# Dilated attention feeding a Strassen MoE on one Trainium2 core: two differences of h in places of their own, seven weight places, and the last attention visits moved

## The chip, the cores and the metric

The kernel runs on one core of a Trainium2 chip. The metric is the device time of one execution in microseconds (us); lower is better. Before the change three runs took 957.64, 956.73 and 954.7 us, median 956.73.

## The reference

```python
# attention: q, k, v are [8, 8, 576, 64]; the first 4 heads use mask_plain, the others mask_dil
mask_plain = (rel >= 0) & (rel < 32)
mask_dil = (rel >= 0) & (rel < 128) & (rel % 4 == 0)
scores = np.where(masks, scale * q @ k.T, -1e9)
attn = softmax(scores);  attn_out = attn @ v
# x: [4608, 512]; w_gate, w_val: [512, 1536]; w_out: [1536, 512]
g = x @ w_gate
silu = g * (1.0 / (1.0 + np.exp(-g)))
return silu * (x @ w_val) @ w_out
```

The 4608 tokens are 8 batches of 576; a token's x is the attention output of its 8 heads. Everything is float32.

## The kernel before

Tokens run along the free dimension (columns), features along the partitions. A float32 product is made of three TensorE passes over a high and a low half of each operand, so every operand needs a "split": ScalarE copies the rounded high half (a CAST or COPY), and VectorE (DVE) or GpSimd (POOL) subtracts it to get the low half. TensorE (PE) is fed by five queues: its own, DVE, ScalarE (ACT), POOL and SyncE (SP). The order in which instructions stand on each engine is set by a scheduler from the order in the code and its own estimate of times; on the chip each engine then works its queue strictly in that order.

The program has two parts.

- **Plain part**: 4 chunks of 384 columns, in 48 steps (gate, value, output product). Beside it, combinations of the weights are formed and written to DRAM as 63 "pieces" of 512 KB.
- **Strassen part**: 3 chunks (0, 1, 2) of 1024 columns, each as 2 x 2 blocks with NT = 7 products in place of 8. A chunk is 126 "slots". The first 84 are the **gate stage**: for each of NP = 6 pairs of feature blocks (i), 7 products (t), 2 slots each, one for gate and one for value. `gated` forms the four blocks of h, `hq[a, b, i]`, as sums of products come in: the last (0,1) after t = 6. The other 42 slots are the **out stage**: 7 products of 6 steps. One slot is 6 matmuls of 128x512 in the gate stage and 6 in the out stage too.

What else runs in the Strassen part:

- **Pieces.** Each product reads one piece (two i of the out stage share one). `ask` starts their transfers from POOL's queue into a ring of NAT places at `M_RING`; `next_piece(n)` stands behind the product that reads piece n and asks for piece n + NAT - 1, whose place was left by piece n - 1.
- **h for the out stage.** `h_split` makes the high and low halves of the operand of an out product: for t = 0, 1, 5, 6 a block of h, for t = 3 and 4 the differences hq[0,1] - hq[0,0] and hq[1,1] - hq[0,1], which `h_mix` forms on POOL in place, in hq[0,0] and hq[0,1]. In place means that it must stand behind the split of t = 0, which reads hq[0,0]. So `h_mix(i)` stands at the end of i for i = 0, 1, 2; those of 3 and 4 stand with the splits of i = 5; that of 5 behind the stage. For t = 2 two more differences are formed on DVE (`tt` on line 736, called from `h_split`). Low halves alternate between POOL (even i) and DVE (odd i); nine places (HS) hold them, so a split is made 8 steps ahead of its product.
- **Sums of x.** `x_step` 0 to 10 forms the seven x operands of the next chunk from its four blocks b11, b12, b21, b22, with 128x1024 operations on DVE and ACT; steps 0 to 7 and 10 stand in slots 104 to 124 of the chunk ahead, 8 and 9 in the first slots of the chunk itself.
- **Attention visits.** 46 packs of attention are worked off in between. A visit m has two ends: A (PE: `results` of m-1, `scores` of m; then DVE `norm` of m-1, line 404, and `shift` of m, lines 365 to 368; ACT `exps`, line 373) and, some slots later, B (PE: `turn_y` of m-1, line 411, which needs norm, and `turn_e` of m, line 377, which needs exps; ACT copies to x). PE works in order too, so if norm or exps is late at B, PE stands still. Chunk 0 of the Strassen part needs packs up to 25, chunk 1 those from 26 to 35, chunk 2 those from 36 to 45. Before, visits 27 to 36 stand in chunk 0 with A in slots 2 to 94; visits 37 and 38 in slots 106 and 119 of its out stage, between the sums of x; 39 to 46 in slots 5 to 94 of chunk 1. Chunk 2 has none.

Of the kernel before, what the change touches and what calls it, by code (L numbers as in the profile page):

```python
# [25 lines left out]
NF = DFF // P  # L26
NK = DM // P
WB = 3 * DM
NP = NF // 2
# [15 lines left out]
CS = 512  # L45
# [7 lines left out]
PIECE = 1024  # L53
NPG = NT * NP
NPIECE = NPG + NT * NP // 2


ORDER = (2, 0, 3, 1)
# [61 lines left out]
NPK = len(PACKS)  # L120
# [14 lines left out]
def attention_moe(ctx, tc, qkb, vb, w, masks, ident, out):  # L135
    nc = tc.nc
# [15 lines left out]
    M_X0 = M_RAW + 8 * WU  # L152
    M_W = M_X0 + 2 * NK * CH
    M_RING = M_W + NT * 4 * CS
    M_HQ = M_RING + 10 * PIECE
    assert M_HQ + 4 * NP * CS <= M_W + 2 * WB * NF
    M_LOW = M_RAW + PIECE
    M_OT = M_LOW + 2 * PIECE + CS
    assert M_OT + 4 * CH + 2 * CS <= M_X0
# [3 lines left out]

    pieces = tc.dram_tile([NPIECE, P, PIECE], F32, name="pieces")

    def at(o, n, dt=F32):

        assert o % 8 == 0
        key = o, n, dt
        if key not in named:  # L170
            k = n * 4 // mybir.dt.size(dt)
            named[key] = nc.alloc_sbuf_tensor_at(f"at{o}_{n}_{dt.name}", [P, k], dt, offset=origin + 4 * o).ap()
        return named[key]
# [395 lines left out]
    NSLOT = 21 * NP  # L569
    SB = NPLAIN * NB  # L570
# [3 lines left out]
    def visits(m, a, b):  # L574
        assert a not in visit and b not in visit
        visit[a], visit[b] = ("A", m), ("B", m)


    M1 = 4 * NPLAIN + 10
# [4 lines left out]
    for m in range(13, M1 + 1):  # L584
        a = SB - 75 + 49 * (m - 13) // 10
        visits(m, a, a + 3)
    for n in range(9):
        a = SB + 2 + 92 * n // 9
        visits(M1 + 1 + n, a, a + 6)
    for m in range(M1 + 10, NPK + 1):  # L590
        a = SB + 94 + NSLOT * (m - M1 - 10) // 10
        visits(m, a, a + 7)

    def attend(now):
        what, m = visit.get(now, ("", 0))
# [94 lines left out]

    NAT = 10
    taken = {}
    asked = 0
    NC = NCS
# [1 line left out]
    def ask(n):  # L698

        nonlocal asked  # L700
        while asked < min(n, NPIECE * NC):
            taken[asked] = at(M_RING + PIECE * (asked % NAT), PIECE, F32R)
            nc.gpsimd.dma_start(out=taken[asked], in_=pieces[asked % NPIECE])  # L703
            asked += 1

    def next_piece(n):

        taken.pop(n)
        ask(n + NAT)


    xs = [[at(M_W + 2 * CS * (2 * t + l), 2 * CS, F32R).rearrange("p (k c) -> p k c", k=2) for l in range(2)]
          for t in range(NT)]
    hq = {(a, t, i): at(M_HQ + CS * (4 * i + 2 * a + t), CS) for a in range(2) for t in range(2) for i in range(NP)}

    x1 = at(M_X0 + 4 * CS, 2 * CS).rearrange("p (k c) -> p k c", k=2)
    HS = 9
# [17 lines left out]
    def tt(engine, out, a, b, op=ALU.subtract):  # L735
        engine.tensor_tensor(out=out, in0=a, in1=b, op=op)  # L736
# [16 lines left out]
    def h_split(n):  # L753

        t, i = divmod(n % (NT * NP), NP)
        if t == 2:
            src = h2_ring()
            tt(nc.vector, src, hq[1, 1, i], hq[0, 0, i])
            tt(nc.vector, hq[1, 0, i], hq[1, 0, i], src)
        else:  # L760
            src = (hq[0, 0, i], hq[1, 0, i], None, hq[0, 0, i], hq[0, 1, i], hq[1, 0, i], hq[1, 1, i])[t]
        o = at(hs_at(n), 2 * CS, F32R).rearrange("p (l c) -> p l c", l=2)
        nc.scalar.copy(out=o[:, 0], in_=src)  # L763
        tt((nc.gpsimd, nc.vector)[i % 2], o[:, 1], src, o[:, 0])
        hs[n] = o

    def h_mix(i):

        tt(nc.gpsimd, hq[0, 0, i], hq[0, 1, i], hq[0, 0, i])
        tt(nc.gpsimd, hq[0, 1, i], hq[1, 1, i], hq[0, 1, i])  # L770


    banks = [[bank_g, bank_v], bank_o[:2], bank_o[2:]]

# [24 lines left out]
    def gated(i, t):  # L799
        if t not in SUMS:  # L800
            return
        a, b = SUMS[t][0]
        g = total(t, 0, g_ring)
        f = f_ring()
        nc.scalar.activation(out=f, in_=g, func=AF.Tanh, scale=0.5)  # L805
        v = total(t, 1, v_ring)
        nc.vector.scalar_tensor_tensor(out=f, in0=f, scalar=1.0, in1=g, op0=ALU.add, op1=ALU.mult)  # L807
        nc.vector.scalar_tensor_tensor(out=hq[a, b, i], in0=f, scalar=0.5, in1=v, op0=ALU.mult, op1=ALU.mult)  # L808

    def outs(ci, t, i, r):  # L810
        w = taken[NPIECE * ci + NPG + NP // 2 * t + i // 2]
# [22 lines left out]
    for s in range(NS):  # L834
        ci, f = divmod(s, NF)
        W = 2 * s
        w_upto(L=W + 3, H=W + 4, E=W + 6)
        gv_mm(ci, f, 0)
        act_tanh(s)
        attend(3 * s)  # L840
        dve_u(s)
        mix_to(2 * (s - NF) + 1)
        with tc.issue_after(last["h"].ins):
            w_upto(T=W + 5, B=W + 5)
        w_upto(L=W + 4, H=W + 5, E=W + 7)
        gv_mm(ci, f, 1)
        attend(3 * s + 1)
        dve_h(s)
        h_hi(s)
        with tc.issue_after(last["h"].ins):  # L850
            w_upto(T=W + 6, B=W + 6)
        if s > 0:
            out_mm(s - 1)
        h_lo(s)
        if s > 0 and f == 0:
            out_store(ci - 1)
        attend(3 * s + 2)

        mix_to(2 * (s - NF) + 2)
        if ci == NPLAIN - 1:  # L860
            if f >= 9:
                ask([4, 7, NAT - 1][f - 9])
            for n in {5: (0,), 6: (1,), 7: (2,), 8: (3,), 10: (4, 5), 11: (6, 7)}.get(f, ()):
                x_step(n)


    for ci in range(NC):
        base = SB + NSLOT * ci
        first = n_out(ci, 0, 0)
        for i in range(NP):  # L870
            for n in range(NT):
                for r in range(2):
                    gate_val(ci, i, n, r)
                    if ci == 0 and i == 0 and n == 1 and r == 1:
                        out_mm(NS - 1)
                        out_store(NPLAIN - 1)
                    attend(base + 2 * (NT * i + n) + r)
                gated(i, SEQ[i][n])
                next_piece(NPIECE * ci + NT * i + n)
                if i == 0 and n < 3:  # L880
                    if n < 2 or ci == 0:
                        x_step((8, 9, 10)[n])
                if i == NP - 1:
                    for k in {1: (3, 4), 2: (5, 6), 3: (7, 8)}.get(n, ()):
                        h_split(first + k)
                        if k < 5:
                            h_mix(k)
            if i < 3:
                h_split(first + i)
                h_mix(i)  # L890
        h_mix(NP - 1)
        for t in range(NT):
            for i in range(NP):
                n = n_out(ci, t, i)
                for r in range(2):
                    outs(ci, t, i, r)
                    if i == NP - 1:
                        out_done(ci, t, r)
                if first < n and n - 1 + HS < n_out(ci + 1, 0, 0):
                    h_split(n - 1 + HS)  # L900
                if i % 2 == 1:
                    next_piece(NPIECE * ci + NPG + NP // 2 * t + i // 2)
                slot = 2 * NPG + NP * t + i
                attend(base + slot)
                if ci + 1 < NC and slot > 102 and slot % 2 == 0:
                    k = (slot - 104) // 2
                    if k < 8 or k == 10:
                        x_step(k)
# [44 lines left out]
```

## Time and profile before

| what | value |
|---|---|
| median of 3 runs | 956.73 us |
| profiled execution, its time | 954.66 us |
| its span | 952.9 us |
| mean granted TensorE clock | 0.995 |
| PE busy | 932.4 us (98%) |
| DVE busy | 642.1 us (67%) |
| ACT busy | 391.3 us (41%) |
| POOL busy | 347.0 us (36%) |

The profiled execution is 2.07 us under the median of the runs shown and 1.76 us above its own span. Line numbers (L736) are those of the code above; a line that is a helper's, as `tt` at L736, stands for all who call it. In lists of instructions the columns are start, duration, engine, line, operation, output <- inputs, count, and in brackets the idle time ahead and who ended it.

### The profile page before, as it was taken

The numbers are of one execution on the slowest core, as the hardware profiler recorded it, in microseconds if no ns is written. First come the engines' busy times: TensorE is split into PE (matmuls) and PEld (weight loads), VectorE is DVE, ScalarE is ACT, GpSimd is POOL, SyncE is SP. The second block draws the span as 40 slices with busy tenths as digits, with TensorE's granted clock in tenths as the row PEclk, the third lists the DMA queues.
The fourth block names the chain that finished last, engine by engine and source line by source line (L and its number), as shares of the span: only waits on it lengthen the run. The fifth ranks groups of instructions, "written<-read, shape, count | busy, mean of one in ns | idle before, by whom it ended". The sixth has DMA issues, their size and how long they took to land.

```text
span 952.9 us, 21913 instructions
## 1 busy us (share of the span) xinstructions
PE 932.4 (98%) x9204; PEld 814.8 (86%) x9204; DVE 642.1 (67%) x1008; ACT 391.3 (41%) x687; POOL 347.0 (36%) x364
## 2 busy tenths in 40 slices
PE   7899999999999999999999999999998899999998
PEld 5799999999999999888887888888886788888886
DVE  4766566667667755767579884666699735656972
ACT  4886322333233334333334643333445433333452
POOL 0776311111111131233145752232267623334681
PEclk9999999999999999999999999999999899999999
DMA  9985166566767691777777678677754586665571
GB/s 369 329 283 195 40 213 225 177 221 219 241 228 245 216 358 63 250 221 234 215 220 235 220 239 288 218 211 217 238 171 163 178 264 193 187 195 176 177 221 66
DMA packets 75249, 205.25 MB, mean 215 GB/s; under 512 B 7568, under 2 KB 23824, under 8 KB 75152
## 3 DMA queue, kind: packets, MB, share of 16 engines
q0 software_dynamic: 27216, 99.10, 34.4%
q1 hardware_dynamic: 35696, 65.07, 19.2%
q10 hardware_dynamic: 12240, 39.70, 12.5%
q8 instruction: 72, 1.18, 0.5%
q14 instruction: 25, 0.20, 0.1%
HBM read 161.37 MB, written 42.47 MB: 214 GB/s over the span
## 4 chain that ended last, share of the span: by engine, by line
PE 87%; DVE 8%; ACT 2%; issue 1%; DMA 0%; ACTq 0%; DVEq 0%
PE bo L779 29%; PE bo L495 10%; PE bv L458 10%; PE bg L458 10%; PE bv L779 10%; PE bg L779 10%; PE two L393 3%; DVE at_float L736 2%; PE two L353 2%; DVE at_float32r L736 2%; PE two L377 2%; PE two L411 2%; DVE at_float L807 1%; DVE at_float L808 1%; DMA at_bfloat<-masks 0%
## 5 line engine op out<-in xcount | busy, mean ns | idle before, releaser
L779 PE MATMUL bo<-at_float32r 128*128 128x512 f32 x1296 | 311.5, 394 | 0.2 <-DVE at_float L736 0.2
L779 PEld LDWEIGHTS bo<-at_float32r 128*128 128x128 f32 x1296 | 243.2, 189 | 52.3 <-DVE at_float L736 0.4
L703 POOL DMA_DIRECT2D at_float32r<-pieces x189 | 103.7, 549 | 251.3 <-PE bo L779 145.1
L736 DVE TENSOR_TENSOR at_float<-bo,at_float 128x512 f32<-128x512 f32 x168 | 113.5, 686 | 112.4 <-ACT at_float L784 57.9
L487 POOL TENSOR_TENSOR at_float32r<-at_float,at_float32r 128x384 fp32r<-128x384 f32 x48 | 54.9, 1144 | 218.0 <-PE bo L495 175.4
L779 PE MATMUL bg<-at_float32r 128*128 128x512 f32 x486 | 129.5, 392 | 0.8 <-DVE at_float32r L736 0.8
L779 PE MATMUL bv<-at_float32r 128*128 128x512 f32 x486 | 129.5, 393 | 0.0
L736 DVE TENSOR_TENSOR at_float32r<-at_float,at_float32r 128x512 fp32r<-128x512 f32 (+1 forms) x84 | 99.4, 1201 | 42.9 <-ACT at_float32r L763 28.5
L736 POOL TENSOR_TENSOR at_float32r<-at_float,at_float32r 128x512 fp32r<-128x512 f32 x63 | 95.5, 1516 | 63.3 <-ACT at_float32r L763 60.4
L458 PE MATMUL bg<-at_float32r,at_float32r 128*128 128x384 f32 x576 | 110.8, 339 | 2.1 <-DVE at_float L472 1.3
L458 PE MATMUL bv<-at_float32r,at_float32r 128*128 128x384 f32 x576 | 110.1, 338 | 0.0
L495 PE MATMUL bo<-at_float32r,at_float32r 128*128 128x384 f32 x576 | 110.1, 338 | 0.0
L779 PEld LDWEIGHTS bg<-at_float32r 128*128 128x128 f32 x486 | 90.5, 188 | 20.2 <-DVE at_float32r L736 1.2
L779 PEld LDWEIGHTS bv<-at_float32r 128*128 128x128 f32 x486 | 90.4, 188 | 19.4
L763 ACT CAST at_float32r<-at_float 128x512 fp32r<-128x512 f32 x126 | 75.7, 621 | 68.5 <-DVE at_float L736 21.5
L458 PEld LDWEIGHTS bg<-at_float32r,at_float32r 128*128 128x128 f32 x576 | 99.9, 188 | 3.7 <-POOL at_float32r L277 1.1
L495 PEld LDWEIGHTS bo<-at_float32r,at_float32r 128*128 128x128 f32 x576 | 100.2, 188 | 0.9
L458 PEld LDWEIGHTS bv<-at_float32r,at_float32r 128*128 128x128 f32 x576 | 99.8, 188 | 0.8
L805 ACT ACTIVATE at_float<-at_float 128x512 f32<-128x512 f32 x72 | 45.6, 634 | 86.9 <-DVE at_float L736 86.9
L472 DVE SCALAR_TENSOR_TENSOR at_float<-at_float,bg 128x384 f32<-128x384 f32 x48 | 26.6, 553 | 75.7 <-ACT at_float L467 75.7
L784 ACT COPY at_float<-bg 128x512 f32<-128x512 f32 x63 | 36.9, 586 | 81.3 <-PE bg L779 81.3
L277 POOL TENSOR_TENSOR at_float32r<-at_int,at_float32r 128x768 fp32r<-128x768 f32 x24 | 46.0, 1925 | 39.9 <-ACT at_float32r L273 39.7
(80 smaller groups left out, 980.0 us busy)
## 6 DMA issues: line engine op xcount, KB each, us to landing
at_float32r<-pieces POOLq DMA_DIRECT2D x189, 512.0 KB, 4.3
pieces<-at_float32r SPq DMA_DIRECT2D x126, 256.0 KB, 4.9
at_int<-w SPq DMA_DIRECT2D x24, 768.0 KB, 6.3
at_float<-vb ACTq DMA_DIRECT2D x28, 390.0 KB, 4.9
at_float<-vb ACTq DMA_DIRECT2D x14, 520.0 KB, 5.4
at_float<-qkb ACTq DMA_DIRECT2D x14, 448.0 KB, 5.8
out<-at_float SPq DMA_DIRECT2D x24, 256.0 KB, 4.5
at_float<-qkb ACTq DMA_DIRECT2D x10, 544.0 KB, 6.9
```

The lines of the kernel that those rows point to most:

```text
L277: nc.gpsimd.tensor_tensor(out=lo, in0=wst.pop(u).bitcast(F32), in1=hi, op=ALU.subtract)
L393: nc.tensor.matmul(out=two[BQ * j:BQ * j + BQ, h, (D + 1) * g:(D + 1) * (g + 1)], lhsT=t[r, BQ * i:BQ * i + BQ], rhs=v[r, i, :], start=Tru ...
L458: nc.tensor.matmul(out=bank[:, :CH], lhsT=wcol(f, o, low), rhs=x[ORDER[j]], start=n == 0, stop=n == len(ops) - 1)
L472: last["h"] = nc.vector.scalar_tensor_tensor(out=t, in0=t, scalar=1.0, in1=bank_g[:, :CH], op0=ALU.add, op1=ALU.mult)
L487: nc.gpsimd.tensor_tensor(out=hl, in0=hst[i][0], in1=hst[i][1], op=ALU.subtract)
L495: nc.tensor.matmul(out=bank_o[j][:, :CH], lhsT=wcol(f, 2 * DM + P * j, low), rhs=x, start=f == 0 and low == 0 and x is hh, stop=f == NF - ...
L703: nc.gpsimd.dma_start(out=taken[asked], in_=pieces[asked % NPIECE])
L736: engine.tensor_tensor(out=out, in0=a, in1=b, op=op)
L763: nc.scalar.copy(out=o[:, 0], in_=src)
L779: nc.tensor.matmul(out=bank, lhsT=w, rhs=x, start=first and n == 0 and t in FRESH, stop=last and n == len(ops) - 1, skip_group_check=True)
L784: nc.scalar.copy(out=kept[KEPT[t]][r], in_=banks[0][r][:, :CS])
L805: nc.scalar.activation(out=f, in_=g, func=AF.Tanh, scale=0.5)
```

## The change

1. `h1[i]`, a new place per i, takes hq[0,1] - hq[0,0]; hq[0,1] - in place still - takes the other difference. Both are issued in `gated` as soon as t = 6 of that i is done, ahead of `next_piece`. `h_mix` and its calls go. Product 3 reads h1.
2. Six places of h are paid for by three of the ring: NAT is 7 in place of 10; the first transfers, asked for in the plain part, are 6 pieces in place of 9.
3. Visits 37 and 38 leave the out stage of chunk 0. Chunk 1 now has ten visits (37 to 46) with A in the same slots as in chunk 0, 2 to 94; in the Strassen part B comes 6 slots behind A everywhere, where it was 7 for the visits from 36 on.

```diff
+NAT = 7
-    M_HQ = M_RING + 10 * PIECE
-    assert M_HQ + 4 * NP * CS <= M_W + 2 * WB * NF
+    M_HQ = M_RING + NAT * PIECE
+    assert M_HQ + 5 * NP * CS <= M_W + 2 * WB * NF
...
-    for n in range(9):
-        a = SB + 2 + 92 * n // 9
-        visits(M1 + 1 + n, a, a + 6)
-    for m in range(M1 + 10, NPK + 1):
-        a = SB + 94 + NSLOT * (m - M1 - 10) // 10
-        visits(m, a, a + 7)
+    for m in range(M1 + 1, NPK + 1):
+        c, n = divmod(m - M1 - 1, 10)
+        a = SB + NSLOT * c + 2 + 92 * n // 9
+        visits(m, a, a + 6)
...
-    hq = {(a, t, i): at(M_HQ + CS * (4 * i + 2 * a + t), CS) for a in range(2) for t in range(2) for i in range(NP)}
+    hq = {(a, t, i): at(M_HQ + CS * (5 * i + 2 * a + t), CS) for a in range(2) for t in range(2) for i in range(NP)}
+    h1 = [at(M_HQ + CS * (5 * i + 4), CS) for i in range(NP)]
...
-            tt(nc.vector, src, hq[1, 1, i], hq[0, 0, i])
+            tt(nc.vector, src, hq[1, 1, i], h1[i])
...
-            src = (hq[0, 0, i], hq[1, 0, i], None, hq[0, 0, i], hq[0, 1, i], hq[1, 0, i], hq[1, 1, i])[t]
+            src = (hq[0, 0, i], hq[1, 0, i], None, h1[i], hq[0, 1, i], hq[1, 0, i], hq[1, 1, i])[t]
...
-    def h_mix(i):
-
-        tt(nc.gpsimd, hq[0, 0, i], hq[0, 1, i], hq[0, 0, i])
-        tt(nc.gpsimd, hq[0, 1, i], hq[1, 1, i], hq[0, 1, i])
...
         nc.vector.scalar_tensor_tensor(out=hq[a, b, i], in0=f, scalar=0.5, in1=v, op0=ALU.mult, op1=ALU.mult)
+        if t == 6:
+            tt(nc.gpsimd, h1[i], hq[0, 1, i], hq[0, 0, i])
+            tt(nc.gpsimd, hq[0, 1, i], hq[1, 1, i], hq[0, 1, i])
...
-                ask([4, 7, NAT - 1][f - 9])
+                ask([3, 5, NAT - 1][f - 9])
...
                         h_split(first + k)
-                        if k < 5:
-                            h_mix(k)
             if i < 3:
                 h_split(first + i)
-                h_mix(i)
-        h_mix(NP - 1)
```

Each engine's order was taken from both built programs. In the rows below a tile is named by its place in SBUF, its size in words, its type and a number. The rows at three places of chunk 1 follow; L736 is `tt` before, L735 the same after.

POOL, from the split of step 4 in the last i of the gate stage, before. `at50880` and `at52928` are hq[0,0] of i = 3 and 4, `at51392` and `at53440` their hq[0,1]:

```order
L736 TENSOR_TENSOR at21184_1024_float32r_519<-at52928_512_float32_536,at21184_1024_float32r_519 128x512
L703 DMA at42688_1024_float32r_4587<-pieces_57 128x1024
L736 TENSOR_TENSOR at50880_512_float32_535<-at51392_512_float32_541,at50880_512_float32_535 128x512
L736 TENSOR_TENSOR at52928_512_float32_536<-at53440_512_float32_542,at52928_512_float32_536 128x512
L736 TENSOR_TENSOR at51392_512_float32_541<-at52416_512_float32_553,at51392_512_float32_541 128x512
L736 TENSOR_TENSOR at53440_512_float32_542<-at54464_512_float32_554,at53440_512_float32_542 128x512
L703 DMA at43712_1024_float32r_4605<-pieces_57 128x1024
L736 TENSOR_TENSOR at23232_1024_float32r_521<-at45760_512_float32_544,at23232_1024_float32r_521 128x512
```

The same place after, from the mixing of i = 3 on; `at51392` and `at53952` are now h1 of i = 3 and 4:

```order
L735 TENSOR_TENSOR at51392_512_float32_559<-at49856_512_float32_541,at49344_512_float32_535 128x512
L701 DMA at34496_1024_float32r_4492<-pieces_57 128x1024
L735 TENSOR_TENSOR at49856_512_float32_541<-at50880_512_float32_553,at49856_512_float32_541 128x512
L701 DMA at35520_1024_float32r_4494<-pieces_57 128x1024
L701 DMA at36544_1024_float32r_4496<-pieces_57 128x1024
L701 DMA at37568_1024_float32r_4539<-pieces_57 128x1024
L701 DMA at38592_1024_float32r_4541<-pieces_57 128x1024
L701 DMA at39616_1024_float32r_4587<-pieces_57 128x1024
L701 DMA at40640_1024_float32r_4605<-pieces_57 128x1024
L735 TENSOR_TENSOR at53952_512_float32_560<-at52416_512_float32_542,at51904_512_float32_536 128x512
L735 TENSOR_TENSOR at52416_512_float32_542<-at53440_512_float32_554,at52416_512_float32_542 128x512
L735 TENSOR_TENSOR at21184_1024_float32r_519<-at51904_512_float32_536,at21184_1024_float32r_519 128x512
```

The four mixing instructions that stood together stand in pairs, those of i = 3 one i (7 pieces) earlier, those of i = 4 ahead of the split of step 4.

DVE, in the last i of the gate stage, before. `at16064` and `at17088` are b11 and b12 of x, `at19136` their difference (x_step 2), `at27328` its low half (x_step 3); the rows that read `bo2` to `bo0` are the sums of products 4 and 5 for the last blocks of h:

```order
L736 TENSOR_TENSOR at22208_1024_float32r_520<-at54976_512_float32_537,at22208_1024_float32r_520 128x512
L736 TENSOR_TENSOR at24256_1024_float32r_522<-at47808_512_float32_545,at24256_1024_float32r_522 128x512
L736 TENSOR_TENSOR at19136_1024_float32_556<-at17088_1024_float32_103,at16064_1024_float32_102 128x1024
L736 TENSOR_TENSOR at27328_1024_float32r_525<-at19136_1024_float32_556,at26304_1024_float32r_524 128x1024
L736 TENSOR_TENSOR at10944_512_float32_4723<-bo2_509,at6648_512_float32_561 128x512
L736 TENSOR_TENSOR at12992_512_float32_4774<-bo3_513,at7160_512_float32_562 128x512
L807 SCALAR_TENSOR_TENSOR at13504_512_float32_4725<-at13504_512_float32_4725,at10944_512_float32_4723 128x512
```

The same place after:

```order
L735 TENSOR_TENSOR at22208_1024_float32r_520<-at54464_512_float32_537,at22208_1024_float32r_520 128x512
L735 TENSOR_TENSOR at24256_1024_float32r_522<-at45248_512_float32_545,at24256_1024_float32r_522 128x512
L735 TENSOR_TENSOR at10944_512_float32_4723<-bo2_509,at6648_512_float32_567 128x512
L800 SCALAR_TENSOR_TENSOR at13504_512_float32_4725<-at13504_512_float32_4725,at10944_512_float32_4723 128x512
L735 TENSOR_TENSOR at12992_512_float32_4774<-bo3_513,at7160_512_float32_568 128x512
L735 TENSOR_TENSOR at10944_512_float32_4723<-at43200_512_float32_550,at43712_512_float32_556 128x512
L801 SCALAR_TENSOR_TENSOR at56000_512_float32_555<-at13504_512_float32_4725,at12992_512_float32_4774 128x512
```

The two 128x1024 rows of the x sums are gone from ahead of the sums of h.

DVE, at the last visit of chunk 1 (46, A in slot 94, only norm is left of it: L402 to L404 before, L403 to L405 after), before. `at33472` from `at11456` is the split of step 17, the last with t = 2:

```order
L736 TENSOR_TENSOR at56000_512_float32_549<-at56000_512_float32_549,at11456_512_float32_4770 128x512
L736 TENSOR_TENSOR at21184_1024_float32r_519<-at16064_1024_float32_102,at20160_1024_float32r_518 128x1024
L736 TENSOR_TENSOR at33472_1024_float32r_531<-at11456_512_float32_4770,at33472_1024_float32r_531 128x512
L736 TENSOR_TENSOR at23232_1024_float32r_521<-at7672_1024_float32_104,at22208_1024_float32r_520 128x1024
L736 TENSOR_TENSOR at9720_1024_float32r_5078<-at46784_512_float32_533,at9720_1024_float32r_5078 128x512
L402 TENSOR_SCALAR at728_8_float32_3160<-two_497 128x8
L403 RECIPROCAL at728_8_float32_3160<-at728_8_float32_3160 128x8
L404 TENSOR_TENSOR at3576_512_float32_874<-two_497,at728_8_float32_3160 128x2x4x64
```

The same place after:

```order
L735 TENSOR_TENSOR at55488_512_float32_549<-at55488_512_float32_549,at11456_512_float32_4770 128x512
L735 TENSOR_TENSOR at33472_1024_float32r_531<-at11456_512_float32_4770,at33472_1024_float32r_531 128x512
L735 TENSOR_TENSOR at23232_1024_float32r_521<-at7672_1024_float32_104,at22208_1024_float32r_520 128x1024
L735 TENSOR_TENSOR at19136_1024_float32_562<-at17088_1024_float32_103,at16064_1024_float32_102 128x1024
L735 TENSOR_TENSOR at27328_1024_float32r_525<-at19136_1024_float32_562,at26304_1024_float32r_524 128x1024
L735 TENSOR_TENSOR at9720_1024_float32r_5080<-at46272_512_float32_557,at9720_1024_float32r_5080 128x512
L403 TENSOR_SCALAR at728_8_float32_3166<-two_497 128x8
L735 TENSOR_TENSOR at12480_512_float32_4727<-bo0_501,at4600_512_float32_563 128x512
L404 RECIPROCAL at728_8_float32_3166<-at728_8_float32_3166 128x8
L735 TENSOR_TENSOR at12992_512_float32_4774<-bo1_505,at5112_512_float32_564 128x512
L405 TENSOR_TENSOR at3576_512_float32_880<-two_497,at728_8_float32_3166 128x2x4x64
```

The two rows of x_step 2 and 3 now stand here, and two sums of the first out product (from `bo0` and `bo1`) stand between the rows of norm.

In the out stage of chunk 0 PE's row of instructions has no scores, results or turns any more after slot 100, and has two visits more in the gate stage of chunk 1; PE's instructions are the same in kind and number.

More of the change, by code (lines that the diff above doesn't have):

```diff
@@ L689, in mix_stage @@
                     mix_out(n)
-    NAT = 10
     taken = {}
```

## Prediction

> **What bounds the kernel now.** I read the page first, then the Strassen part by stretches, PE's waits, and the chain around each of them.
>
> ```profile
> span 952.9 us, 21913 instructions
> PE 932.4 (98%) x9204; PEld 814.8 (86%) x9204; DVE 642.1 (67%) x1008; ACT 391.3 (41%) x687; POOL 347.0 (36%) x364
> PE 87%; DVE 8%; ACT 2%; issue 1%; DMA 0%; ACTq 0%; DVEq 0%
> ```
>
> PE is the bound; 8% of the chain runs through DVE. The change keeps every PE instruction, so all that it can move is time in which PE stands still or runs at a lower clock. The stretches are chunk 0, 1 and 2 of the Strassen part, and PE's waits over the three of them (PE waited, for whom, total us, times, longest):
>
> ```profile
> core 0: us, PE busy (x) PEld busy (x) DVE busy (x) ACT busy (x) POOL busy (x), PEclk, DMA share, GB/s
> 375.00:578.00 203.00, 200.88 (x2158) 164.85 (x2157) 144.90 (x220) 84.90 (x156) 84.91 (x96) 1.00 0.73 229
> 578.00:777.00 199.00, 193.13 (x1632) 157.69 (x1631) 141.48 (x195) 81.77 (x145) 82.86 (x96) 0.98 0.68 209
> 777.00:953.00 176.00, 171.88 (x756) 141.58 (x755) 106.23 (x140) 64.58 (x109) 74.14 (x87) 0.99 0.59 178
> ...
> PE two L411 <- DVE at_float L404: 3.7, 1, 3.7
> PE two L377 <- ACT at_float L373: 3.3, 2, 2.1
> PE bg L779 <- DVE at_float32r L736: 0.8, 1, 0.8
> ```
>
> That is all there is to win: 7.8 us of waits, and a clock under 1.00 in chunk 1. Nothing in PE waits for a piece. The four waits in PE's list:
>
> ```profile
> 521.95 0.66 PE L377 MATMUL two<-at_float,at_float 128*128 128x128 f32 x4 [2.12 <-ACT at_float L373]
> ...
> 716.72 0.55 PE L377 MATMUL two<-at_float,at_float 128*128 128x128 f32 x3 [1.19 <-ACT at_float L373]
> ...
> 735.84 0.73 PE L779 MATMUL bg<-at_float32r 128*128 128x512 f32 x2 [0.75 <-DVE at_float32r L736]
> 740.95 1.11 PE L411 MATMUL two<-at_float,at_float 128*128 128x128 f32 x4 [3.68 <-DVE at_float L404]
> ```
>
> One is in chunk 0 (visit 35, B in slot 89); three are in chunk 1, all at the turn from gate stage to out stage: visit 45, the split of step 17, visit 46. The clock behind the last pause:
>
> ```profile
> 739.40:746.20 6.80, 5.25 (x15) 4.29 (x16) 6.73 (x11) 1.79 (x4) 2.16 (x2) 0.50 0.63 205
> ```
>
> Half clock for 6.80 us, of which PE stood still for the first 1.55; the remaining 5.25 us held work worth half of that, so 2.6 us are lost. The pause of 2.12 us in chunk 0 left the clock at 1.00. Chunk 1 thus pays 1.19 + 0.75 + 3.68 + 2.6 = 8.2 us, chunk 0 pays 2.1.
>
> **Why chunk 1 is later than chunk 0.** The chain of chunk 1, from DVE's side:
>
> ```profile
> 699.84 2.37 DVE at_float L736
> ...
> 702.28 1.06 ACT at_float32r L739
> ...
> 703.37 1.23 DVE at_float32r L736
> ...
> 716.61 1.69 DVE at_float32r L736
> ...
> 719.50 3.39 DVE at_float32r L736 x2
> ...
> 730.52 9.34 DVE at_float32r L736 x4
> ```
>
> The first three are x_step 2 and 3, which the order of before puts ahead of the sums of the last h: 2.37 + 1.06 + 1.23 = 4.7 us on DVE's queue, with DVE idle while ACT makes the high half. Ahead of them POOL had worked off four mixings in one run:
>
> ```profile
> 691.50 5.92 POOL L736 TENSOR_TENSOR at_float<-at_float,at_float 128x512 f32<-128x512 f32 x4
> ```
>
> From 703 to 740 the chain stays on DVE but for one stop on ACT. What makes it worse is that a DVE subtraction of 128x512 that takes 0.68 us by itself takes 1.7 when one of POOL runs at the same time (716.61, 719.50 x2). The last run of four (730.52, two of them 128x1024) stands ahead of norm of visit 46, and PE waits for that. Chunk 0 has the same instructions, and its x_step 2 and 3 stand just ahead of that norm:
>
> ```profile
> 525.91 1.21 DVE L736 TENSOR_TENSOR at_float32r<-at_float,at_float32r 128x1024 fp32r<-128x1024 f32 x1
> ...
> 531.71 2.98 DVE L736 TENSOR_TENSOR at_float32r<-at_float,at_float32r 128x1024 fp32r<-128x1024 f32 x2 [1.12 <-ACT at_float32r L739]
> ...
> 535.04 0.69 DVE L404 TENSOR_TENSOR at_float<-two,at_float 128x512 f32<-128x512 f32 x1
> ...
> 540.38 0.60 PE L411 MATMUL two<-at_float,at_float 128*128 128x128 f32 x4
> 540.82 0.49 PE L377 MATMUL two<-at_float,at_float 128*128 128x128 f32 x3
> ```
>
> There norm was done at 535.73, 4.65 us before PE came to B. So with nearly the same work one chunk has 4.65 us to spare and the other misses by 3.7.
>
> **The change, part by part.**
>
> *Visits.* Two leave the out stage of chunk 0, where no wait of PE stands, and two enter the gate stage of chunk 1, where visits wait for nothing before slot 88: 0 either way. PE's time for them is only moved from one chunk to the other. What counts is what the scheduler makes of it: pack 43 now arrives later in chunk 1, so x_step 2 and 3 go behind the sums of the last h, as in chunk 0. That takes 4.7 us off DVE at 700 to 704, and puts 128x1024 work ahead of norm of visit 46, which chunk 0 shows to be bearable. I therefore take chunk 0 of before as the picture of chunk 1 after:
> - visit 45: 1.19 becomes 2.12 (A in slot 83, B in 89, as visit 35 had): +0.9;
> - step 17: 0.75 goes, since chunk 0 has no such wait: -0.75;
> - visit 46: B is a slot earlier. A slot is six matmuls:
>
> ```profile
> 760.56 16.43 PE bo L779 x72
> ...
> L736 DVE TENSOR_TENSOR at_float<-bo,at_float 128x512 f32<-128x512 f32 x168 | 113.5, 686 | 112.4 <-ACT at_float L784 57.9 <-PE bo L779 44.4 <-ACT at_float L805 8.7
> ```
>
> 16.43 / 12 = 1.37 us a slot. Of chunk 0's 4.65 us I take 1.37, and two sums of 0.69 that now stand between the rows of norm, 1.38: 1.9 us are left. The wait goes: -3.68, and the half clock with it: -2.6. What is late next is visit 45.
>
> Visit 36 in chunk 0 has exps too, ended at 538.94 by this row:
>
> ```profile
> 538.41 0.53 ACT L373 ACTIVATE at_float<-at_float 128x384 f32<-128x384 f32 x1 [4.01 <-DVE at_float L368]
> ```
>
> - chunk 0: visit 35 has the same rows between A and B as before: 0. Visit 36 has B a slot earlier; its norm keeps 3.3 us, its exps, which PE came to at 540.82, keep 1.88 - 1.37 = 0.5: 0, though thinly.
>
> *Differences of h.* Thirty-six mixings before, thirty-six after, on the same engine. Those of i = 3 and 4 leave the run of 5.92 us for the ends of their own i, where PE has no wait. The earliest the new pairs could cost is a piece asked for later, since `next_piece` stands behind them: two of about 1.5 us (5.92 / 4) and DVE's lag. Ends: a gain of 2 us if DVE is freed from two slowed subtractions at 697 to 701, a loss of 0; I take 0, since those subtractions lie ahead of x_step 2 and 3, whose going frees DVE at the same place.
>
> *Seven places.* A piece is asked for when the one before the current is done, so it has 6 x 2 slots = 16.4 us from the request to its product, where it had 24.7. Against that:
>
> ```profile
> at_float32r<-pieces POOLq DMA_DIRECT2D x189, 512.0 KB, 4.3
> ...
> 525.21 6.54 POOL L736 TENSOR_TENSOR at_float32r<-at_float,at_float32r 128x512 fp32r<-128x512 f32 x1 [4.15 <-ACT at_float32r L763]
> ```
>
> 4.3 us to land and the longest time for which one POOL instruction holds up the requests, 6.5: 16.4 - 10.8 = 5.6 us are left. Cost 0; two such delays in a row would use it up. At the start six pieces lie ready in place of nine, 16 us ahead: 0.
>
> *The sum*: +0.9 - 0.75 - 3.68 - 2.6 = -6.1 us. The profiled execution would take 954.66 - 6.1 = 948.5 us. It stands 2.07 us under the median; against the median of 956.73, which is what a measurement compares, I predict 950.6.
>
> **Rivals.** Two rows of DVE for them, from chunk 0 and chunk 2:
>
> ```profile
> 518.02 2.55 DVE L736 TENSOR_TENSOR at_float32r<-at_float,at_float32r 128x512 fp32r<-128x512 f32 x1
> ...
> 894.29 7.02 DVE L736 TENSOR_TENSOR at_float<-at_float,at_float 128x512 f32<-128x512 f32 x3
> ```
>
> 1. *All pauses go* (visit 45 and 35 too): 2.12 + 1.19 + 0.75 + 3.68 + 2.6 = 10.3 us, 946.4. For it: without the run of four mixings POOL is ahead, and a subtraction of 2.55 us, 1.9 more than its own 0.68, stands in chunk 0 just ahead of the last of shift (518.02), so that one meeting less with POOL would do away with most of the 2.12. Against it: those rows are in the order unchanged.
> 2. *The lag stays* (no change): which of DVE and POOL gets in first is a matter of tenths of a microsecond, and chunk 1 may meet POOL as often as before. With only step 17 and the 4.7 us of x_step relieved, a pause of 2 to 4 us at visit 46 stays with its clock: 955 to 957.
> 3. *Slower*: norm of visits 36 and 46 loses the race. In chunk 2 one DVE subtraction stood through four of POOL's: 7.02 less two of 0.68 is 5.7 us for one. If chunk 1 lags as before, the earlier B and the two sums add 1.37 + 1.38 to the wait: 3.68 + 2.75 = 6.4, plus clock 2.6, step 17 0.75, visit 45 2.12, together 11.9 in place of 8.2: +3.7, 960.4. It decides from the point where DVE is more than 1.9 us later, relative to PE, than chunk 0 was; it comes out slower than before only beyond some 8 us of lag.
> 4. *Pieces come late*: with over 5.6 us of further delay of POOL's requests, PE waits 1 to 3 us at the out stage of each chunk: up to 956.
>
> The Trainium skill has a rule on the first three, SBUF — State Buffer, section "Who interferes with whom": a VectorE instruction with two SBUF inputs and a GpSimd instruction that reads SBUF take a shared port by turns, and the loser stands still for the whole of the other's instruction. By that rule a meeting costs DVE at most one of POOL's instructions, and the earlier B of visit 46 would need two more of them than chunk 0 met before PE waits at all; rival 3 would drop to a chance of some 0.03 at the same 960.4. The 7.02 us row, in which one subtraction outlasts several of POOL's, says otherwise, so I leave it at 0.09.
>
> **How the numbers follow.** Forecast, a gain of 3 to 9 us: 0.53, its own range 947.7 to 953.7. All pauses gone: 0.15. The lag stays: 0.20. Slower by the norm: 0.09. Late pieces: 0.03. A measurement of this kernel tells about 0.3%, 2.9 us (its runs span 2.94), from no change. Faster 0.53 + 0.15 + 0.01 = 0.69; same 0.20 + 0.02 = 0.22; slower 0.09. The range reaches from a little below the first rival (946.4, and the runs' 2 us under the median) to between rivals 2 and 3: 945.5 to 958.5.
>
> **What would show it.** In the changed kernel's waits of PE from the first Strassen product on: turn_y on norm (line 411 on 404, one line on) gone or under 1 us, turn_e on exps (377 on 373) about 4 us in two, no product waiting for a split or a piece. PEclk 1.00 in chunks 0 and 1. POOL without a run of four mixings. Chunks 0 and 1 together about 396 us where they had 402, chunk 2 unchanged. I am wrong if a pause over 3 us stands at visit 36 or 46, or if a product waits for a transfer.

## The result and the profile after

The changed kernel takes 946.38 us (median of 4 runs, 946.28 to 947.31); the kernel before, timed beside it, 956.07 (4 runs, 954.7 to 957.64). The ratio is 0.990, 95% interval 0.9882 to 0.9918: faster by 9.7 us. The forecast was 950.6, its own range 947.7 to 953.7, the whole range 945.5 to 958.5. The sign and the place of the gain were right and the size was too small. The time came out where rival 1 had put it (946.4), but not by rival 1's way: two of the pauses that it takes away are still there.

The page after, head and PE's waits from the first Strassen product on:

```profile
span 944.6 us, 21916 instructions
PE 929.7 (98%) x9204; PEld 812.9 (86%) x9204; DVE 633.3 (67%) x1008; ACT 391.9 (41%) x687; POOL 346.1 (37%) x364
...
PE two L378 <- ACT at_float L374: 2.8, 2, 1.6
```

Of the five losses that the prediction counted (turn_y on norm, two of turn_e on exps, the split of step 17, half clock) the two of turn_e on exps are left. Its two places, and PE at B of visits 36 and 46, where PE now comes without a stop; the ACT row is exps of visit 36:

```profile
521.21 0.66 PE L378 MATMUL two<-at_float,at_float 128*128 128x128 f32 x4 [1.63 <-ACT at_float L374]
...
537.67 0.53 ACT L374 ACTIVATE at_float<-at_float 128x384 f32<-128x384 f32 x1 [3.98 <-DVE at_float L369]
...
538.30 0.60 PE L412 MATMUL two<-at_float,at_float 128*128 128x128 f32 x4
538.74 0.49 PE L378 MATMUL two<-at_float,at_float 128*128 128x128 f32 x3
...
717.04 0.66 PE L378 MATMUL two<-at_float,at_float 128*128 128x128 f32 x4 [1.17 <-ACT at_float L374]
...
733.67 0.60 PE L412 MATMUL two<-at_float,at_float 128*128 128x128 f32 x4
```

The next rows are DVE's: ahead of the last row of shift of visits 35 (first row) and 45 (second row), and at visit 46 of chunk 1: x_step 2 and 3 (third and fourth row, 128x1024, the latter grouped with the next subtraction) now stand behind the sums of h, and norm still ends at 731.31 + 0.67 = 731.98, 1.69 us ahead of PE's 733.67.

```profile
517.24 2.59 DVE L735 TENSOR_TENSOR at_float32r<-at_float,at_float32r 128x512 fp32r<-128x512 f32 x1
...
713.53 1.32 DVE L735 TENSOR_TENSOR at_float<-at_float,at_float 128x512 f32<-128x512 f32 x1
...
724.75 1.21 DVE L735 TENSOR_TENSOR at_float<-at_float,at_float 128x1024 f32<-128x1024 f32 x1
...
727.07 2.98 DVE L735 TENSOR_TENSOR at_float32r<-at_float,at_float32r 128x1024 fp32r<-128x1024 f32 x2 [1.11 <-ACT at_float32r L738]
...
731.31 0.67 DVE L405 TENSOR_TENSOR at_float<-two,at_float 128x512 f32<-128x512 f32 x1
```

POOL's run of four mixings (5.92 us at 691.50) is gone. The pair of i = 4 (first row) stands alone, and that of i = 5 (last) behind its own blocks; between them a split's subtraction by itself:

```profile
685.85 2.67 POOL L735 TENSOR_TENSOR at_float<-at_float,at_float 128x512 f32<-128x512 f32 x2 [1.23 <-DVE at_float L801]
...
690.75 1.29 POOL L735 TENSOR_TENSOR at_float32r<-at_float,at_float32r 128x512 fp32r<-128x512 f32 x1
...
709.02 3.44 POOL L735 TENSOR_TENSOR at_float<-at_float,at_float 128x512 f32<-128x512 f32 x2 [2.27 <-DVE at_float L403]
```

The windows over the three chunks (columns as in the prediction; the same times from the span's start as before, so the last holds 8 us of the end, where PE has nothing left):

```profile
375.00:578.00 203.00, 201.37 (x1986) 165.16 (x1987) 141.72 (x210) 86.43 (x156) 86.48 (x98) 1.00 0.73 224
578.00:777.00 199.00, 197.83 (x1853) 162.31 (x1847) 137.69 (x207) 85.46 (x152) 83.53 (x97) 1.00 0.73 225
777.00:953.00 176.00, 163.57 (x719) 134.53 (x718) 104.52 (x136) 60.47 (x103) 72.82 (x87) 0.99 0.57 174
```

In the window of chunk 1 PE's busy time goes from 193.13 of 199 us to 197.83, and the clock from 0.98 to 1.00. Where the time went, by the first product of chunk 0 and of chunk 2, before and then after:

```profile
375.10 1.55 PE L779 MATMUL bg<-at_float32r 128*128 128x512 f32 x6
...
776.82 1.52 PE L779 MATMUL bg<-at_float32r 128*128 128x512 f32 x6
```
```profile
374.85 1.32 PE L772 MATMUL bg<-at_float32r 128*128 128x512 f32 x5
...
768.45 1.30 PE L772 MATMUL bg<-at_float32r 128*128 128x512 f32 x5
```

Chunks 0 and 1 took 776.82 - 375.10 = 401.72 us and take 768.45 - 374.85 = 393.60: 8.12 less, of 8.29 between the two profiled executions (954.66 and 946.37). The plain part and chunk 2 give nothing.

### The profile page after: what moved, and what is told of

It is laid out like the page before. It is cut to its first block, busy times and chain, and to the rows that moved or that the text cites. A ratio compares the mean times of both kernels' runs of the same rounds, so it can differ in the third digit from the quotient of the medians.

```text
span 944.6 us, 21916 instructions
## 1 busy us (share of the span) xinstructions
PE 929.7 (98%) x9204; PEld 812.9 (86%) x9204; DVE 633.3 (67%) x1008; ACT 391.9 (41%) x687; POOL 346.1 (37%) x364
## 4 chain that ended last, share of the span: by engine, by line
PE 91%; DVE 5%; ACT 2%; issue 1%; DMA 0%; ACTq 0%; DVEq 0%
PE bo L772 30%; PE bg L772 11%; PE bv L772 11%; PE bo L496 10%; PE bv L459 10%; PE bg L459 10%; PE two L394 3%; PE two L354 2%; PE two L378 2%; DVE at_float L735 2%; PE two L412 1%; DVE at_int L263 0%; DMA at_bfloat<-masks 0%; DVE at_float L800 0%; DVE at_float L801 0%
## 5 line engine op out<-in xcount | busy, mean ns | idle before, releaser
L772 PE MATMUL bo<-at_float32r 128*128 128x512 f32 x1296 | 308.0, 391 | 0.0
L735 DVE TENSOR_TENSOR at_float<-bo,at_float 128x512 f32<-128x512 f32 x168 | 113.7, 685 | 109.8 <-ACT at_float L777 59.8
L735 DVE TENSOR_TENSOR at_float32r<-at_float,at_float32r 128x512 fp32r<-128x512 f32 (+1 forms) x84 | 99.2, 1205 | 40.3 <-ACT at_float32r L762 24.8
L735 POOL TENSOR_TENSOR at_float32r<-at_float,at_float32r 128x512 fp32r<-128x512 f32 x63 | 96.7, 1536 | 44.6 <-ACT at_float32r L762 43.3
```

What stands on the lines that cost most here:

```text
L772: nc.tensor.matmul(out=bank, lhsT=w, rhs=x, start=first and n == 0 and t in FRESH, stop=last and n == len(ops) - 1, skip_group_check=True)
```

## The experiments

Which part of the change does it? The theories, as the expectations letter them: A, the order alone (x_step 2 and 3 behind the sums of h); B, the mixings (a shorter run on POOL, fewer meetings with DVE); C, visits taken out from among x's sums. The kernel before was timed again beside each group of experiments: 956.13 us beside visits_only, places_only, sums_tied and packs_early, 956.07 beside two_in_out, nat5, nat4 and turn_late, 955.31 beside mix_on_dve and visits_late. All rows of waits below are PE's from the first Strassen product on (for whom: us, times, longest). Ratios are to the kernel before of the same group, as 95% intervals.

### visits_only: the new visit slots alone

```diff
 # kernel before
-    for n in range(9):
-        a = SB + 2 + 92 * n // 9
-        visits(M1 + 1 + n, a, a + 6)
-    for m in range(M1 + 10, NPK + 1):
-        a = SB + 94 + NSLOT * (m - M1 - 10) // 10
-        visits(m, a, a + 7)
+    for m in range(M1 + 1, NPK + 1):
+        c, n = divmod(m - M1 - 1, 10)
+        a = SB + NSLOT * c + 2 + 92 * n // 9
+        visits(m, a, a + 6)
```

> The kernel before with the visits' new slots alone: ten places for weights, differences of h formed in place, the run of four mixings on POOL kept. Theory A (the order of x_step 2 and 3 on DVE in chunk 1, which follows from the slots of the visits, is the cause): all of the gain, 946 to 949 us, PE's waits in the Strassen part 2.5 to 4.5 us, the wait of turn_y on norm at visit 46 gone, clock 1.00 in chunk 1. Theory B (the run of four mixings sets DVE back, and its going is the gain): the run is still there, so 953 to 957 us with the wait of 3.7 us.

Measured 948.24 us, ratio 0.9908 to 0.9933.

```profile
PE two L377 <- ACT at_float L373: 3.8, 2, 2.1
...
523.48:526.89 3.41, 3.41 (x11) 2.64 (x10) 3.41 (x6) 2.88 (x8) 0.68 (x1) 0.50 0.61 221
```

Norm and the split are gone from the waits, with the mixings still in place: 7.9 us from the slots alone. The two waits left are 2.12 us at visit 35 and 1.68 at visit 45. The second row is a window behind visit 35's pause: half clock for 3.41 us.

### places_only: the places and the ring of seven alone

The changed kernel with the old lines of the visits, the diff above the other way round.

> The changed kernel with the visits' old slots: seven places for weights, differences of h in places of their own, mixings in pairs. Theory A: x_step 2 and 3 are back ahead of the sums of the last h, so 953 to 957 us, with a wait of 2 to 5 us of turn_y on norm at visit 46 and about 2.5 us of half clock behind it. Theory B: 946 to 950 us.

Measured 951.87 us, ratio 0.9946 to 0.9973. Its waits; x_step 2 of chunk 1 on DVE there; and, from the kernel before, the split on POOL that x_step 2 met:

```profile
PE two L412 <- DVE at_float L405: 2.4, 1, 2.4
PE bg L774 <- DVE at_float32r L737: 1.6, 1, 1.6
PE two L378 <- ACT at_float L374: 1.6, 1, 1.6
...
698.54 1.23 DVE L737 TENSOR_TENSOR at_float<-at_float,at_float 128x1024 f32<-128x1024 f32 x1
```
```profile
699.80 1.30 POOL L736 TENSOR_TENSOR at_float32r<-at_float,at_float32r 128x512 fp32r<-128x512 f32 x1
```

The order of before is kept, and norm is still late, by 2.4 us in place of 3.68, with 3.41 us of half clock behind it. But x_step 2 takes 1.23 us there, where it took 2.37 before: POOL's run of four (691.50 to 697.42) had pushed a split back to 699.80, into x_step 2; here POOL's splits are done ahead of it. So neither theory's range holds alone (A expected 953 us or more, B 950 or less), and B, with the seven places, is worth some 4 us by itself.

### sums_tied: the order alone

Kernel before; x_step 2 and 3 may not be issued ahead of the last block of h, and nothing else in the code changes.

```diff
-        nc.vector.scalar_tensor_tensor(out=hq[a, b, i], in0=f, scalar=0.5, in1=v, op0=ALU.mult, op1=ALU.mult)
+        last["g"] = nc.vector.scalar_tensor_tensor(out=hq[a, b, i], in0=f, scalar=0.5, in1=v, op0=ALU.mult,
+                                                   op1=ALU.mult)
...
-                    if k < 8 or k == 10:
+                    if k in (2, 3):
+                        with tc.issue_after(last["g"].ins):
+                            x_step(k)
+                    elif k < 8 or k == 10:
                         x_step(k)
```

> The kernel before with one tie: x_step 2 and 3 of the next chunk may not stand ahead of the last block of h (DVE's and ACT's order change at this one place; PE's, POOL's and the visits' slots are those of before). Theory A: most of the gain without any of the three edits, 946 to 950 us, waits of PE at most 4 us. Theory B, and theory C (the visits among the sums of x in the out stage of chunk 0 are what costs): no change, 955 to 957 us.

Measured 948.48 us, ratio 0.9904 to 0.993.

```profile
PE two L377 <- ACT at_float L373: 2.1, 1, 2.1
PE two L411 <- DVE at_float L404: 1.2, 1, 1.2
```

With old visits, old mixings and ten places, two rows moved on DVE's queue bring 7.7 us. In the trace x_step 2 stands 37 places later on DVE, x_step 3 39; a few neighbouring rows change places too, ACT's order changes around them, and POOL's is that of before. This is the mechanism that the prediction named, by itself.

### packs_early: the changed kernel with the order put back

```diff
-        visits(m, a, a + 6)
+        if c == 1:
+            a = SB + NSLOT + (2, 11, 20, 30, 39, 48, 58, 68, 81, 94)[n]
+        visits(m, a, a + 6 + (c == 1 and n > 6))
```

The visits of chunk 1 come earlier, the last three in their old slots with B 7 slots behind A, so that the eighth pack is there in time for x_step 2 and 3 to stand ahead of the sums of h again.

> The changed kernel, but the visits of chunk 1 stand in slots 2, 11, 20, 30, 39, 48, 58, 68, 81, 94, so that the packs for x_step 2 and 3 come as early as before; no visit stands among the sums of x. Theory A: x_step 2 and 3 go ahead of the sums of the last h again and the wait comes back: 951 to 957 us, turn_y on norm 2 to 5 us. Theories B and C: as the changed kernel, 946 to 947 us.

Measured 951.52 us, ratio 0.9939 to 0.9963.

```profile
PE two L412 <- DVE at_float L405: 3.7, 1, 3.7
PE two L378 <- ACT at_float L374: 1.6, 1, 1.6
PE bg L774 <- DVE at_float32r L737: 0.2, 1, 0.2
```

Some 5 us of the gain are lost again, and the norm's pause of 3.7 us is back in a kernel that has all of the change but these slots. The pause is as long as before although the mixings are apart, but it is nearly the only one: PE's pauses at this turn are 0.2 + 3.65 = 3.9 us here, and were 1.19 + 0.75 + 3.68 = 5.6 before, where the first two brought PE to norm later.

### two_in_out: visits 37 and 38 back among the sums of x

```diff
-        visits(m, a, a + 6)
+        if m in (37, 38):
+            a = SB + 106 + 13 * (m - 37)
+        visits(m, a, a + 6)
```

> The changed kernel with visits 37 and 38 back in the out stage of chunk 0 (slots 106 and 119), among the sums of x; the other visits of chunk 1 stay in their new slots, so x_step 2 and 3 stay behind the sums of the last h. Theory A (their place on DVE is what counts): as the changed kernel within 1 us, 945.5 to 947.5. Theory C (a visit among the sums of x costs by itself): 948 to 951 us, with a wait of PE in the out stage of chunk 0.

Measured 947.02 us, ratio 0.9898 to 0.9924; the only row of waits reads as in the changed kernel (2.8, 2, 1.6). Theory C falls: that no visits stand among x's sums is worth nothing by itself that these runs could tell.

### nat5 and nat4: fewer weight places still

```diff
-NAT = 7
+NAT = 5
...
-                ask([3, 5, NAT - 1][f - 9])
+                ask([2, 3, NAT - 1][f - 9])
```

nat4 has `NAT = 4` and `ask([1, 2, NAT - 1][f - 9])`.

> The changed kernel with five places for weights. A piece is then asked for 4 products, 10.9 us, ahead. By the working of the prediction (4.3 us to land, 6.5 us for the longest hold-up on POOL) 0.1 us is left at the tightest: 946 to 948 us, PE waiting for pieces 0 to 1 us in all. If transfers were hidden with much to spare: 946.4. If every request were late: over 955.

> The changed kernel with four places for weights, 3 products or 8.2 us ahead. By the same working some 8 pieces at the turns to the out stages come up to 2.7 us late, PE waits about 3 us in chunk 2, 2 in chunk 0, under 1 in chunk 1: 950 to 954 us. If the lead were never what counts: 946.4.

Measured: nat5 948.44 us (0.9914 to 0.9938), nat4 956.89 (1.0003 to 1.0022), both above what was expected. The first row is nat5's, the others nat4's:

```profile
PE bg L772 <- DMA at_float32r<-pieces: 0.3, 1, 0.3
```
```profile
PE bg L772 <- DMA at_float32r<-pieces: 5.9, 3, 2.7
PE two L378 <- ACT at_float L374: 2.8, 2, 1.6
PE bo L772 <- DMA at_float32r<-pieces: 0.5, 1, 0.5
```

By the prediction's reckoning ((NAT - 1) x 2 slots of 1.37 us) a piece is asked for 11 us ahead with five places and 8.2 with four; less 10.8 that leaves 0.2 and -2.6. Of the counts that were run, five is the first at which PE waits, and at four its longest wait for a piece is 2.7 us. nat4's profiled execution (953.98 us, the lowest of its runs) is 7.6 us over the changed kernel's and shows 6.4 us of such waits; why its median lies 3 us higher stays open, and so does why nat5's lies 2 us over the changed kernel's with 0.3 us more of waits. With seven places PE waits for no piece; a ring of four would have eaten the whole gain.

### mix_on_dve: the mixings off POOL

```diff
-            tt(nc.gpsimd, h1[i], hq[0, 1, i], hq[0, 0, i])
-            tt(nc.gpsimd, hq[0, 1, i], hq[1, 1, i], hq[0, 1, i])
+            tt(nc.vector, h1[i], hq[0, 1, i], hq[0, 0, i])
+            tt(nc.vector, hq[0, 1, i], hq[1, 1, i], hq[0, 1, i])
```

> The changed kernel with the twelve mixings of each chunk on DVE in place of POOL. They take 0.68 us each on DVE, and POOL's took up to 1.1 us from a DVE subtraction that they met. If meeting POOL is what sets DVE back at the turn, the two of i = 5, 1.36 us more on DVE's queue but two meetings fewer, come out even or better: 944.5 to 947.5 us, turn_e on exps 1.5 to 4 us in two waits. If POOL's subtractions cost DVE nothing, DVE is 1.4 us later at visits 35 and 45: each wait about 1.4 us longer, 949 us.

Measured 947.13 us, ratio 0.9891 to 0.9924.

```profile
PE two L378 <- ACT at_float L374: 2.1, 1, 2.1
...
517.09 0.67 DVE L735 TENSOR_TENSOR at_float32r<-at_float,at_float32r 128x512 fp32r<-128x512 f32 x1
...
539.11 0.55 PE L378 MATMUL two<-at_float,at_float 128*128 128x128 f32 x3 [2.08 <-ACT at_float L374]
...
539.99:543.40 3.41, 3.41 (x10) 2.63 (x9) 3.06 (x4) 3.26 (x9) 2.13 (x3) 0.50 0.74 243
```

DVE does 36 subtractions more and the kernel is less than 1 us slower. The pauses at visits 35 and 45 are gone: the subtraction ahead of the last row of shift of visit 35 takes 0.67 us where it took 2.59. There it had met two splits that stood behind the mixings on POOL's queue; without the mixings POOL is at no split then (514.71 to 516.00, and again from 520.91). One pause of 2.08 us comes at visit 36, where 0.54 us were to spare, with half clock behind it; two waits were expected. On balance, mixings on POOL cost DVE about as much as doing them itself.

### turn_late and visits_late: B later where DVE is late

```diff
 # turn_late: the changed kernel; visits_late: the same edit on visits_only
-        visits(m, a, a + 6)
+        visits(m, a, a + (8 if n > 7 else 6))
```

Visits 35, 36, 45 and 46 get B two slots (2.7 us) later.

> The changed kernel with B two slots later for the last two visits of chunks 0 and 1 (35, 36, 45, 46): A in slots 83 and 94, B in 91 and 102. If the two waits that are left (turn_e on exps, 1.63 and 1.17 us) are DVE's lag against a fixed B, two slots of 1.37 us take both away: 943 to 945 us. If DVE's lag only moves on to the next wait (norm of the last visit, a split, exps of 36): 945.5 to 947.

> The kernel before with the new slots of the visits and B two slots later for visits 35, 36, 45 and 46: differences of h in place, ten places for weights. If all that is left to win is PE's waits at the turn and the clock behind them: no waits over 0.5 us, 943.5 to 945.5 us, the same as with places of their own for the differences. If the run of four mixings still sets DVE back by more than the two slots cover: waits of 1 us or more at visits 36, 45 or 46, and 946 us or more.

Measured: turn_late 944.14 us (943.25 to 944.89), ratio 0.9864 to 0.9893; visits_late 944.96 (944.23 to 945.26), ratio 0.9873 to 0.9902. PE's waits, turn_late and then visits_late:

```profile
PE two L394 <- ACT at_float L438: 0.2, 1, 0.2
```
```profile
PE two L393 <- ACT at_float L437: 1.2, 2, 0.8
```

turn_late beats both kernels: 1.1% to 1.4% under the one before. And visits_late, with mixings in place and ten weight places, has nearly all of it: once B stands where norm and exps are done, PE hardly sees DVE's lag any more. Waits of up to 0.8 us are left there, where none over 0.5 was expected. The two intervals overlap, so what the places of their own still add there can't be told from nothing; in the two profiles PE's waits differ by 1.0 us. B later with the old order of x_step 2 and 3 was not run.

## Why the prediction was right, and where it was short

*The mechanism*: right. x_step 2 and 3 ahead of the sums of h made norm of visit 46 late; moving them (sums_tied) gives 7.7 us, putting them back by earlier visits (packs_early) takes 5.1 of 9.7.

*Norm of visit 46*: 1.9 us to spare were forecast, 1.69 are there; -3.68 held, and the half clock's -2.6 with it. *Step 17*: gone, -0.75. *Exps of visit 36*: 0.5 to spare forecast, 538.74 - (537.67 + 0.53) = 0.54 found.

*Visit 45*, the term that was mis-sized most: chunk 0's 2.12 us was copied to it (+0.93), but it is 1.17, as before (1.19). Ahead of its shift the subtraction that meets POOL takes 1.32 us (713.53), where chunk 0's takes 2.55. With the likeness of the chunks went the meeting with POOL, which in chunk 1 is shorter. In all 0.95 us. About half of it is the mixings' doing: with them in place (visits_only) the pause is 1.68 us.

*Visit 35*, costed at 0, went from 2.12 to 1.63: 0.49 us. This too is the mixings' doing. With the run of four in place the pause is 2.12 us (before, visits_only) or 2.15 (sums_tied); with the mixings in pairs it is 1.62 to 1.64 (places_only, packs_early, two_in_out), whatever the visits. The rows are the last of shift of visit 34 on DVE, the split on POOL that it met behind the run of four of chunk 0, and ACT's next copy of a product, before; then DVE's row and ACT's after:

```profile
499.88 1.30 DVE L368 TENSOR_TENSOR at_float<-at_float,at_float 128x384 f32<-128x384 f32 x1
...
499.45 1.30 POOL L736 TENSOR_TENSOR at_float32r<-at_float,at_float32r 128x512 fp32r<-128x512 f32 x1
...
502.74 0.58 ACT L784 COPY at_float<-bg 128x512 f32<-128x512 f32 x1
```
```profile
499.15 0.56 DVE L369 TENSOR_TENSOR at_float<-at_float,at_float 128x384 f32<-128x384 f32 x1
...
501.95 0.59 ACT L777 COPY at_float<-bg 128x512 f32<-128x512 f32 x1 [0.59 <-PE bg L772]
```

After, the copy waits for PE alone. Counted from the first product of chunk 0 it starts at 127.10 us in place of 127.64, and DVE's run of sums of h behind it starts 0.53 us earlier.

*The sum*, -6.1 us, becomes -6.1 - 0.95 - 0.49 = -7.5; chunks 0 and 1 gave -8.1. About 0.6 us stay unassigned; 0.2 of them may be a fifth wait of before, of an out product on DVE, which the prediction's list left out and which is gone too.

*Mixings costed at 0*: wrong by about 1.0 us in this sum, 0.49 at visit 35 and 0.51 at visit 45 (1.68 to 1.17). The reason given for the 0, that x_step 2 and 3 free DVE at the same place by going, fails in chunk 0, where they stood behind the sums of h already; in chunk 1 their going did not free all of it. As a price by itself it is further off: alone (places_only) the mixings bring 4.3 us, alone the order brings 7.7, and both, with the visits, 9.7 and not 12. They are two remedies for one lag, and PE pays only what of a lag goes beyond its slack.

*The step to the median*: the other mis-sized term, 2.07 us. The profiled execution of before lies at the low end of its runs, and its distance to the median was carried over whole to the changed kernel. But that distance goes with the clock, which the change alters: of the 17 runs of before in the second group, the seven with a mean clock of 0.996 took 954.17 to 955.35 us, the five with 0.994 956.07 to 957.34, and none came above 0.996. After has runs at 0.995 to 1.0 within 1.03 us of each other, the profiled one at their median. Without the 2.07 the forecast would have been 948.5.

*Places*: 0 was right. With seven, the tightest piece, asked for at 901.16 and landed at 904.75, is first used at 910.25: 5.5 us to spare, 5.6 forecast. The nearness is partly luck: it was asked for 9.1 us ahead, later than the forecast's worst (16.4 - 6.5 = 9.9), and landed in 3.6 us in place of 4.3.

*Rivals 2 and 3* did not come: DVE never lost more than its slack at visits 36 and 46. The rule that the prediction took from the Trainium skill (SBUF — State Buffer, section "Who interferes with whom") would have set rival 3 low, and the outcome agrees. But the row of 7.02 us, which speaks against one instruction as the most that a meeting costs, still stands, and so does one of POOL after the change, a subtraction of 1.29 us by itself that takes 4.79:

```profile
722.33 4.79 POOL L735 TENSOR_TENSOR at_float32r<-at_float,at_float32r 128x512 fp32r<-128x512 f32 x1 [4.63 <-ACT at_float32r L762]
```

## What to carry to other kernels

When two stretches of a kernel do the same work and one of them waits, compare their queues row by row: here two rows that the scheduler had put 37 and 39 places earlier on DVE cost 7.7 us, and an edit elsewhere that only delayed their input set it right. Where the deadline is itself a place set by hand (here B), try moving it: two slots took away the pauses that were left, and beside that, parting the mixings added nothing that these runs could tell. And gains that relieve one lag don't add up: price each edit by what is left of the wait when the others are in.

## What was not expected of the hardware

*Half clock after short pauses.* The prediction saw one pause of 2.12 us without loss of clock (before) and put no loss of clock on the pauses of that length in its sum. In three kernels a pause of about that length was followed by 3.41 us at half clock, which loses 1.7: 2.12 us in visits_only and 2.08 in mix_on_dve (windows above), 2.15 in sums_tied:

```profile
522.15 0.66 PE L377 MATMUL two<-at_float,at_float 128*128 128x128 f32 x4 [2.15 <-ACT at_float L373]
...
523.26:526.67 3.41, 3.41 (x10) 2.62 (x9) 3.41 (x6) 3.41 (x8) 1.27 (x1) 0.50 0.41 150
```

A pause of 2.71 us in nat4 had none. The stretches in the Strassen part are 3.41 us long, or about twice that in before. The Trainium skill, TensorE: Matmul & The Clock Gate, Part 1, section "What's actually happening", tells of a free-running window of 3413 ns; the lengths agree. Its section "Why this matters for your kernels" asks for no gap over about 3 us; these runs show that 2.1 us can be too much, and that 2.7 can pass. In these traces what parts the two is how a pause lies in the windows. In each of the twelve profiles the steps of the clock lie whole multiples of 3.413 us apart (in before the second, third and fourth step come 211, 213 and 273 of them behind the first), so that one step places all windows. In the Strassen parts each window at full clock in which PE stood still for 2.08 us or more (six, 2.08 to 3.41 us) was followed by half clock, and none in which it stood still for 1.68 or less. The 2.12 us of before lay 1.12 and 1.01 in two windows, the 2.71 us of nat4 1.46 and 1.24; those of 2.08, 2.12 and 2.15 us lay whole in one. The windows lie differently in every execution (the first edge 0.69 to 3.38 us behind the start of the span), so whether a pause of some 2 to 3 us costs clock can differ from one to the next. Where between 1.68 and 2.08 us the limit lies, no run shows, and no experiment moved a pause within a window.

*A meeting of DVE and POOL can outlast several instructions.* Subtractions of 0.68 us (DVE) and 1.29 us (POOL) were stretched to 5.7 and 4.79 us by a run of the other engine's. Both ended only once that run was over: POOL's fourth subtraction ended at 898.73 + 1.29 = 900.02 and DVE's stretched one at 900.58; DVE's run ended at 724.75 + 1.21 = 725.96 and POOL's stretched one at 727.12. In mix_on_dve DVE did 36 subtractions more and was earlier at visits 35 and 45, with one such meeting less at each.
